# A gated expert on TensorE's column groups, rotations in three operations, and a new order of the first transfers in a state-space kernel

## The chip, the cores and the metric

The kernel runs on one core of one Trainium2 chip. The metric is the time of one execution on the device, in microseconds (us). Two kernels are compared by runs on the same chip, taken in turns. All runs told here gave a correct result. The executions of one kernel in one round spread by 1 to 4 us, and a difference of about 1 us or less is not settled by these runs.

Engines: TensorE (PE in the profile; PEld is its weight loads), VectorE (DVE), ScalarE (ACT), GpSimd (POOL), SyncE (SP). A name such as ACTq is the queue of transfers that this engine issues.

## The reference, cut to what matters

```python
x  = A_x                                  # [1, 2048, 1024], bf16
xn = layernorm(x)
# A: a state-space layer with 1024 complex states, plus a skip
Lam_bar = exp(exp(log_dt) * (Lambda_re + 1j * Lambda_im))
B_bar   = ((Lam_bar - 1) / Lam)[:, None] * (B_re + 1j * B_im)
h[t]    = Lam_bar * h[t-1] + xn[t] @ B_bar.T          # over 2048 tokens
yA      = 2 * (h @ C.T).real + xn * Dskip
# B: one gated expert for the two tokens with the largest r
r   = xn @ w_r
idx = the two largest of r
y   = (silu(xn[idx] @ w_gate) * (xn[idx] @ w_up)) @ w_down * sigmoid(r[idx])   # F = 3584
yB  = xn, with y added at the rows idx
return x + yA + yB
```

## The kernel before

The sequence is cut into 16 chunks of 128 tokens. For each chunk TensorE computes B·x (tile pB), ScalarE copies it out (u), VectorE rotates it (v, four operations), scans it with a real radius (gf), ScalarE casts it (gb), VectorE rotates it back (hT, four operations), and TensorE multiplies by C (pY). VectorE adds the residual (ot). The expert runs between the later chunks.

The order on each engine is fixed when the kernel is built, by a small list scheduler with estimated durations and hand-tuned offsets, cut here:

```python
class Plan:
    def add(self, name, eng, dur, fn, deps=(), key=0.0, takes=(), mb=0.0, lag=0.0): ...
    def run(self): ...     # repeatedly starts the task that can start first; ties by key
    def emit(self): ...    # emits the tasks in that order
```

The start:

```python
nc.scalar.preload_act_table_set("natural_log_exp_and_others")
for c in range(4):                                   # x of chunks 0 to 3, 256 KB each
    (nc.sync if c < 2 else nc.scalar).dma_start(out=xt_tiles[c][:], in_=x2[c * T:(c + 1) * T, :])
prow = moe.tile([5 * PT, 128], BF16, name="prow", tag="row")
for i, src in enumerate((A_Lambda_re, A_Lambda_im, A_log_dt, B_w_r, A_Dskip)):   # 2 KB each
    nc.scalar.dma_start(out=prow[i * PT:(i + 1) * PT, :], in_=src.rearrange("(j i) -> j i", i=128))
# ... after these SyncE issues the transposing loads of B: BT[ri][j], 16 of 256 KB

def par_T():                                         # all five parameters at once
    tab["pP"] = psum.tile([128, 5 * PT], BF16, name="pP", tag="Y", bufs=3)
    nc.tensor.transpose(out=tab["pP"][:], in_=prow[:], identity=ident[0:5 * PT, 0:5 * PT])
```

TensorE's order starts with warm-up products, the transpose of chunk 0 (pT), then pP, pT of chunk 1, and pB. So pP must wait for the last of the five small loads, and everything behind it on TensorE waits with it.

A rotation, and the expert's two inner loops:

```python
def turn_in(c, js=ALLJ):
    # ...
    nc.vector.tensor_tensor(out=m1[:, :, js, :], in0=u, in1=bc(E1c), op=ALU.mult)
    nc.vector.tensor_tensor(out=m2[:, :, js, :], in0=u, in1=bc(E1s), op=ALU.mult)
    nc.vector.tensor_add(out=v[:, 0, js, 2:], in0=m1[:, 0, js, :], in1=m2[:, 1, js, :])
    nc.vector.tensor_sub(out=v[:, 1, js, 2:], in0=m1[:, 1, js, :], in1=m2[:, 0, js, :])

def moe_gateup(n):                                   # 28 visits, 448 products in all
    # ...
    for fl in range(FC // 128):
        ft = fc * (FC // 128) + fl
        for j in range(DT):
            nc.tensor.matmul(out=ms["pG"][:, m, ft, :], lhsT=wt[:, j, fl * 128:(fl + 1) * 128],
                             rhs=ms["xselT"][:, j, :], start=(j == 0), stop=(j == DT - 1))

def moe_down(n):                                     # already in column groups
    # ...
    nc.tensor.matmul(out=ms["pD"][32 * q:32 * q + 2, :], lhsT=ms["guT"][:, ft, :],
                     rhs=wd[:, a, q * DQ:(q + 1) * DQ], ..., tile_position=(0, 32 * q))
```

Of the kernel before, what the change touches and what calls it, by code (L numbers as in the profile page):

```python
# [9 lines left out]
ACT = mybir.ActivationFunctionType  # L10
# [7 lines left out]
T = 128  # L18
# [5 lines left out]
NREP = 4  # L24
ADJUST = {
    ('x', 4): -274.0, ('x', 5): -94.3, ('x', 6): -15.6, ('x', 7): -77.2, ('x', 8): -7.7, ('x', 9): -94.3,
    ('x', 11): -13.0, ('x', 12): -55.3, ('x', 15): -7.1,
    ('B', 0, 0): -906.8, ('B', 0, 1): -906.8, ('B', 1, 0): -986.1, ('B', 1, 1): -986.1, ('B', 2, 0): -728.9,
    ('B', 2, 1): -728.9, ('B', 3, 0): -767.1, ('B', 3, 1): -767.1, ('B', 4, 0): -364.5, ('B', 4, 1): -364.5,
    ('B', 5, 0): -599.0, ('B', 5, 1): -599.0, ('B', 6, 0): -451.9, ('B', 6, 1): -451.9, ('B', 7, 0): -120.1,  # L30
    ('B', 7, 1): -120.1,
    ('C', 0, 0): -47.7, ('C', 0, 1): -47.7,
    ('rstd', 5): 151.6, ('rstd', 10): 59.9,
    ('xnT', 5): -804.0,
    ('sq', 8): 26.9,
    ('apply', 9): 18.3,
    ('sum', 12): -59.1, ('sum', 14): -30.0, ('sum', 15): -21.9,
    ('nmean', 12): 21.0,
    ('nmr', 12): -106.3,
    ('pcol',): 71.2,  # L40
    ('wr',): -7.0,
    ('frq',): 11.2,
    ('ts', 0, 0): -1.2, ('ts', 1, 0): -167.7, ('ts', 0, 1): -1.2, ('ts', 1, 1): -167.7,
    ('E2c', 1): -20.4,
    ('dgD',): -9.1,
    ('u', 0, 0): 22.6, ('u', 0, 1): 22.6, ('u', 0, 2): 22.6, ('u', 0, 3): 22.6, ('u', 0, 4): 22.6, ('u', 0, 5): 22.6,
    ('u', 0, 6): 22.6, ('u', 0, 7): 22.6,
    ('Bu', 4, 0): 52.0, ('Bu', 4, 1): 52.0, ('Bu', 4, 2): 52.0, ('Bu', 4, 3): 52.0, ('Bu', 4, 4): 52.0,
    ('Bu', 4, 5): 52.0, ('Bu', 4, 6): 52.0, ('Bu', 4, 7): 52.0, ('Bu', 5, 0): 110.3, ('Bu', 5, 1): 110.3,
    ('Bu', 5, 2): 110.3, ('Bu', 5, 3): 110.3, ('Bu', 5, 4): 110.3, ('Bu', 5, 5): 110.3, ('Bu', 5, 6): 110.3,  # L50
    ('Bu', 5, 7): 110.3, ('Bu', 6, 0): 125.8, ('Bu', 6, 1): 125.8, ('Bu', 6, 2): 125.8, ('Bu', 6, 3): 125.8,
    ('Bu', 6, 4): 125.8, ('Bu', 6, 5): 125.8, ('Bu', 6, 6): 125.8, ('Bu', 6, 7): 125.8, ('Bu', 7, 0): 186.2,
    ('Bu', 7, 1): 186.2, ('Bu', 7, 2): 186.2, ('Bu', 7, 3): 186.2, ('Bu', 7, 4): 186.2, ('Bu', 7, 5): 186.2,
    ('Bu', 7, 6): 186.2, ('Bu', 7, 7): 186.2,
    ('TI', 0, 0): 1.0, ('TI', 0, 4): 1.0, ('TI', 1, 0): -1.0, ('TI', 1, 4): -1.0, ('TI', 3, 0): -2.4,
    ('TI', 3, 4): -2.4, ('TI', 4, 0): -3.1, ('TI', 5, 0): -3.3,
    ('SC', 0, 0, 0): -8.5, ('SC', 0, 0, 1): -8.5, ('SC', 0, 4, 0): -8.5, ('SC', 0, 4, 1): -8.5,
    ('SC', 3, 0, 0): 38.6, ('SC', 3, 0, 1): 38.6, ('SC', 3, 4, 0): 38.6, ('SC', 3, 4, 1): 38.6,
    ('SC', 5, 0, 0): -51.1, ('SC', 5, 0, 1): -51.1, ('SC', 6, 0, 0): 18.7, ('SC', 6, 0, 1): 18.7,
    ('gb', 0, 0, 0): -13.0, ('gb', 0, 0, 1): -13.0, ('gb', 0, 4, 0): -13.0, ('gb', 0, 4, 1): -13.0,  # L60
    ('TO', 1, 0): -19.8, ('TO', 1, 4): -19.8, ('TO', 4, 0): -85.6, ('TO', 5, 0): 2.5, ('TO', 7, 0): -34.6,
    ('TO', 15, 0): -1.5, ('TO', 15, 4): -1.5, ('TO', 15, 6): -1.5,
    ('cin', 2, 0): -117.9, ('cin', 2, 4): -117.9,
    ('xr', 0): -84.4, ('xr', 1): -75.1, ('xr', 2): -55.1, ('xr', 3): -38.2, ('xr', 4): -53.4, ('xr', 5): -38.7,
    ('xr', 6): -64.2, ('xr', 7): -33.9, ('xr', 8): -35.3, ('xr', 11): -136.6,
    ('Y', 0, 0): 12.6, ('Y', 0, 1): 12.6, ('Y', 0, 2): 12.6, ('Y', 0, 3): 12.6, ('Y', 1, 0): 11.7, ('Y', 1, 1): 11.7,
    ('Y', 1, 2): 11.7, ('Y', 1, 3): 11.7, ('Y', 2, 0): 20.9, ('Y', 2, 1): 20.9, ('Y', 2, 2): 20.9, ('Y', 2, 3): 20.9,
    ('Y', 3, 0): 27.5, ('Y', 3, 1): 27.5, ('Y', 3, 2): 27.5, ('Y', 3, 3): 27.5, ('Y', 9, 0): 121.2,
    ('Y', 9, 1): 121.2, ('Y', 9, 2): 121.2, ('Y', 9, 3): 121.2, ('Y', 10, 0): 157.9, ('Y', 10, 1): 157.9,
    ('Y', 10, 2): 157.9, ('Y', 10, 3): 157.9, ('Y', 12, 0): 192.3, ('Y', 12, 1): 192.3, ('Y', 12, 2): 192.3,  # L70
    ('Y', 12, 3): 192.3, ('Y', 13, 0): 271.5, ('Y', 13, 1): 271.5, ('Y', 13, 2): 271.5, ('Y', 13, 3): 271.5,
    ('out', 2, 0): 14.3, ('out', 2, 1): 14.3, ('out', 8, 0): 81.9, ('out', 8, 1): 81.9,
    ('xa', 5): -18.6,
    ('ADD', 9, 0): 42.2, ('ADD', 9, 1): 42.2,
    ('w', 0): -61.6, ('w', 1): -73.8, ('w', 2): -65.6, ('w', 3): -48.9, ('w', 4): -58.9, ('w', 5): -49.9,
    ('w', 6): -46.1, ('w', 7): -46.5, ('w', 8): -43.0, ('w', 9): -44.6, ('w', 10): -43.9, ('w', 11): -42.3,
    ('w', 12): -45.3, ('w', 13): -45.0, ('w', 14): -44.0, ('w', 15): -44.6, ('w', 16): -45.2, ('w', 17): -45.2,
    ('w', 18): -44.9, ('w', 19): -45.1, ('w', 20): -45.3, ('w', 21): -42.4, ('w', 22): -42.6, ('w', 23): -42.5,
    ('w', 24): -47.4, ('w', 25): -42.6, ('w', 26): -45.3, ('w', 27): -46.3, ('w', 28): -47.2, ('w', 29): -42.6,
    ('w', 30): -39.6, ('w', 31): -43.3, ('w', 32): -27.1, ('w', 33): -39.0, ('w', 34): -14.2, ('w', 35): -24.2,  # L80
    ('w', 36): -15.0,
# [3 lines left out]
class Plan:  # L85
# [3 lines left out]
    FREE = {"PE": 1.35, "DVE": 1.2, "ACT": 4.7, "POOL": 1.8, "SP": 1.65}  # L89
# [80 lines left out]
def kernel(  # L170
# [31 lines left out]
    FC = 256  # L202
    NFC = F // FC
    DQ = D // NREP
    DH = 512
    NDH = D // DH
    x2 = A_x[0]
# [11 lines left out]
    xt_tiles = {c: xin.tile([128, D], BF16, name="xt") for c in range(4)}  # L219
    nc.scalar.preload_act_table_set("natural_log_exp_and_others")  # L220
    for c in range(4):
        (nc.sync if c < 2 else nc.scalar).dma_start(out=xt_tiles[c][:], in_=x2[c * T:(c + 1) * T, :])
    prow = moe.tile([5 * PT, 128], BF16, name="prow", tag="row")
    for i, src in enumerate((A_Lambda_re, A_Lambda_im, A_log_dt, B_w_r, A_Dskip)):
        nc.scalar.dma_start(out=prow[i * PT:(i + 1) * PT, :], in_=src.rearrange("(j i) -> j i", i=128))
# [7 lines left out]
    nc.gpsimd.iota(par_i[:], pattern=[[0, 1]], base=0, channel_multiplier=1)  # L233
    halfpi = consts.tile([128, 1], F32, name="halfpi")
    nc.vector.memset(halfpi[:], math.pi / 2)
    eps_t = consts.tile([128, 1], F32, name="eps_t")
    nc.vector.memset(eps_t[:], EPS)
    first_tok = consts.tile([128, 1], F32, name="first_tok")
# [12 lines left out]
    E1s = consts.tile([128, PT, T], BF16, name="E1s")  # L251
    E2c = consts.tile([128, PT, T], BF16, name="E2c")
# [38 lines left out]
    for c in range(NCH):  # L291
        if c < 4:
            add(("x", c), "none", (3.4, 0.8, 1.5, 0.7)[c], lambda: None, key=c, takes=[("xt", c, [("apply", c)])])
        else:
            add(("x", c), "SP", 0.47 if c > 5 else 1.05, lambda c=c: load_x(c), key=-40 + c, takes=[("xt", c, [("apply", c)])], mb=0.28)
# [106 lines left out]
    NWARM = 36  # L402
    for i in range(NWARM):
        add(("warm", i), "PE", 0.22 if i < 19 else 0.12, keep_clock, [("warm", i - 1)] if i else [], key=100 + i,
            takes=[("pB", "warm", [("warm", NWARM - 1)])])
# [145 lines left out]
    add(("start",), "none", 0.6, lambda: None, key=10)  # L551
# [4 lines left out]
    add(("frq",), "DVE", 0.25, par_frq, [("dt",)], key=-31)  # L556
# [11 lines left out]
    add(("E1s",), "DVE", 0.6, lambda: nc.vector.tensor_copy(out=E1s[:], in_=tab["sf"][:]), [("sin",)], key=-20)  # L568
# [5 lines left out]
    for h, js in enumerate((h0, h1)):  # L574
        for i, (nm, dst) in enumerate((("E2c", E2c), ("E2s", E2s))):
            add(("ts", i, h), "DVE", 0.62, lambda i=i, js=js: table_ts(i, js), [("kappa",), ("sin",)], key=-1.45 + h, takes=[("gb", ("ts", i), [(nm, 1)])])
            add((nm, h), "DVE", 1.05, lambda dst=dst, i=i, js=js: table_E2(dst, i, js), [("ts", i, h), ("cos",)], key=-1.45 + h)
    add(("dgD",), "DVE", 1.2, table_D, [("pcol",)], key=0.1)
    E2D = [(nm, h) for nm in ("E2c", "E2s") for h in range(2)]
    for i in range(3):  # L580
        pl.rings["hT"]["taken"].append((("tab", i), E2D + [("E1c",), ("E1s",), ("ends",)]))
# [53 lines left out]

    def turn_in(c, js=ALLJ):
        n = js.stop - js.start
# [250 lines left out]
    def sel_bn():  # L888
        nc.vector.tensor_scalar_add(out=ms["sig"][:], in0=ms["sig"][:], scalar1=1.0)
        nc.vector.reciprocal(out=ms["sig"][:], in_=ms["sig"][:])  # L890
        ms["mv"] = bn_mean_var(ms["xsel"], 2)
# [142 lines left out]
```

## Time and profile before

| | before |
|---|---|
| time, median of 3 runs | 273.96 us (273.91 to 274.08) |
| span of the profiled execution | 272.3 us |
| TensorE busy | 262.7 us (96%) |
| VectorE busy | 246.1 us (90%) |
| first pB starts | 13.37 us |

The engine table and three rows of the slices, from the profile page of the kernel before. In the engine table, each engine has its busy time and share of the span. In the slices, the span is cut into 40; a digit is tenths, and PEclk is TensorE's granted clock.

```profile
PE 262.7 (96%) x2484; PEld 184.8 (68%) x2504; DVE 246.1 (90%) x360; ACT 145.1 (53%) x239; POOL 107.2 (39%) x204
...
PE   8599999999999999999999999999999999999995
...
DVE  4689999999999999998997999799999998699982
...
PEclk9779999999999999999999999999999999999999
```

TensorE is the fullest engine and VectorE is close. Apart from the last slice, TensorE's only visibly loose slices are at the very start, and there its clock is below full too.

ScalarE's and TensorE's first 14 us of the kernel before, from the timeline (start, length, engine, line, operation, out<-in, count, and in brackets the idle time before it with its releaser; ACTq lines are transfers being issued):

```profile
0.75 0.88 ACTq L222 DMA_DIRECT2D xt<-in_A_x_dram  x2
1.65 0.58 ACTq L225 DMA_DIRECT2D prow<-in_A_Lambda_re_dram  x1
...
5.57 0.28 ACTq L225 DMA_DIRECT2D prow<-in_A_log_dt_dram  x1
7.27 0.30 ACTq L225 DMA_DIRECT2D prow<-in_B_w_r_dram  x1
...
7.96 0.29 ACT L308 ACTIVATE lv<-mv,eps_t 128x1 f32<-128x1 f32 x1 [5.96 <-DMA prow<-in_A_log_dt_dram]
```

```profile
9.13 0.64 PE L385 MATMUL pT<-ident,xn 128*128 128x128 bf16 x8 [1.97 <-DVE xn L358]
11.14 0.19 PE L452 MATMUL pP<-ident,prow 40*128 40x40 bf16 x1 [1.37 <-issue]
...
13.37 1.91 PE L594 MATMUL pB<-xnT,BT 128*128 128x128 bf16 x16
```

ScalarE issued the third and fourth small loads only at 5.57 and 7.27 us, and its first statistic (lv) came behind them. TensorE waited 1.97 us for chunk 0 and 1.37 us before pP, and the first pB started at 13.37 us. The windows view gives the DMA traffic at that time (kernel before; the last two columns are the DMA share and GB/s):

```profile
4.00:6.00 2.00, 2.00 (x21) 2.00 (x20) 1.45 (x4) 0.00 (x0) 0.00 (x0) 1.00 1.12 351
...
10.00:12.00 2.00, 0.86 (x9) 0.84 (x10) 1.97 (x5) 0.82 (x1) 0.40 (x2) 0.50 0.96 188
```

Two groups of the costliest list, kernel before (busy us, mean ns; then idle before):

```profile
L594 PE MATMUL pB<-xnT,BT 128*128 128x256 bf16 (+1 forms) x1040 | 117.9, 272 | 0.0
...
L945 PE MATMUL pG<-xselT,wt 128*128 128x2 bf16 x448 | 13.5, 163 | 0.0
```

The expert's gate and up products (pG) are 448 products of only two moving columns. From start to start, 16 of them take 0.39 us.

### The profile page before, as it was taken

The numbers are of one execution on the slowest core, as the hardware profiler recorded it, in microseconds if no ns is written. First come the engines' busy times: TensorE is split into PE (matmuls) and PEld (weight loads), VectorE is DVE, ScalarE is ACT, GpSimd is POOL, SyncE is SP. The second block draws the span as 40 slices with busy tenths as digits, with TensorE's granted clock in tenths as the row PEclk, the third lists the DMA queues.
The fourth block names the chain that finished last, engine by engine and source line by source line (L and its number), as shares of the span: only waits on it lengthen the run. The fifth ranks groups of instructions, "written<-read, shape, count | busy, mean of one in ns | idle before, by whom it ended". The sixth has DMA issues, their size and how long they took to land.

```text
span 272.3 us, 6159 instructions
## 1 busy us (share of the span) xinstructions
PE 262.7 (96%) x2484; PEld 184.8 (68%) x2504; DVE 246.1 (90%) x360; ACT 145.1 (53%) x239; POOL 107.2 (39%) x204
## 2 busy tenths in 40 slices
PE   8599999999999999999999999999999999999995
PEld 8498898884489555675564896658984577634441
DVE  4689999999999999998997999799999998699982
ACT  1388899996477888996422542214351344213110
POOL 1210066764747563737060196209430515001200
PEclk9779999999999999999999999999999999999999
DMA  6989999998037090714302389969999498632111
GB/s 214 193 180 182 259 199 276 223 268 182 17 96 233 1 195 14 181 42 96 99 0 79 116 231 277 277 188 298 291 264 287 152 337 284 253 137 61 39 39 39
DMA packets 86344, 46.29 MB, mean 170 GB/s; under 512 B 45796, under 2 KB 78570, under 8 KB 86316
## 3 DMA queue, kind: packets, MB, share of 16 engines
q1 hardware_dynamic: 85836, 45.10, 65.9%
q10 hardware_dynamic: 368, 0.53, 0.5%
q8 instruction: 19, 0.31, 0.5%
q0 software_dynamic: 112, 0.27, 0.3%
q14 instruction: 9, 0.07, 0.1%
HBM read 30.68 MB, written 4.20 MB: 128 GB/s over the span
## 4 chain that ended last, share of the span: by engine, by line
PE 49%; DVE 3%; issue 1%
PE pY L774 24%; PE pB L594 17%; PE pG L945 4%; PE pY L767 2%; PE pD L968 1%; DVE gf L666 1%; DVE ot L783 0%; PE pY L776 0%; DVE n L704 0%; DVE n L705 0%; DVE hT L707 0%; PE pI L845 0%; DVE idx L833 0%; DVE top L831 0%; PE pX L905 0%
## 5 line engine op out<-in xcount | busy, mean ns | idle before, releaser
L594 PE MATMUL pB<-xnT,BT 128*128 128x256 bf16 (+1 forms) x1040 | 117.9, 272 | 0.0
L774 PE MATMUL pY<-CT,hT 128*128 128x512 bf16 x492 | 113.9, 379 | 1.3 <-DVE hT L706 0.3
L594 PEld LDWEIGHTS <-BT 128*128 128x128 bf16 x1040 | 99.4, 98 | 12.9 <-issue 0.9
L774 PEld LDWEIGHTS <-hT 128*128 128x128 bf16 x512 | 48.0, 98 | 51.6 <-issue 0.7
L666 DVE TENSOR_TENSOR_SCAN gf<-R,v 128x1040 f32<-128x1040 f32 (+1 forms) x38 | 69.3, 1852 | 0.2 <-POOL v L693 0.2
L682 POOL TENSOR_TENSOR w<-gf,cL 128x8 f32<-128x8 f32 (+1 forms) x38 | 29.0, 763 | 91.7 <-DVE gf L666 79.8
L672 ACT CAST gb<-gf 128x1024 bf16<-128x1024 f32 (+1 forms) x38 | 32.7, 866 | 38.5 <-DVE gf L666 38.3
L600 ACT CAST u<-pB 128x512 bf16<-128x512 f32 x64 | 36.3, 579 | 21.3 <-PE pB L594 21.0
L755 ACT ACTIVATE xa<-xr,nmr_all,rstd_all 128x1024 f32<-128x1024 bf16 x16 | 19.8, 1240 | 35.4 <-DVE ot L783 24.7
L644 DVE TENSOR_TENSOR m<-u,E1c 128x2048 bf16<-128x2048 bf16 (+2 forms) x22 | 20.4, 927 | 6.0 <-ACT u L600 5.5
L783 DVE TENSOR_TENSOR ot<-pY,xa 128x512 bf16<-128x512 f32 x32 | 21.1, 675 | 3.8 <-issue 3.2
L704 DVE TENSOR_TENSOR n<-gb,E2c 128x2048 bf16<-128x2048 bf16 (+2 forms) x22 | 20.4, 926 | 3.8 <-ACT gb L672 3.1
L705 DVE TENSOR_TENSOR n<-gb,E2s 128x2048 bf16<-128x2048 bf16 (+2 forms) x22 | 20.5, 931 | 0.0
L645 DVE TENSOR_TENSOR m<-u,E1s 128x2048 bf16<-128x2048 bf16 (+2 forms) x22 | 20.3, 925 | 0.0
L366 POOL TENSOR_TENSOR nmr_all<-nmean_all,rstd_all 128x1 f32<-128x1 f32 x16 | 8.6, 540 | 29.4 <-ACT rstd_all L309 29.3
L945 PEld LDWEIGHTS <-wt 128*128 128x128 bf16 x448 | 13.5, 96 | 1.9 <-issue 0.2
L683 POOL TENSOR_TENSOR w<-gf,sL 128x8 f32<-128x8 f32 (+1 forms) x38 | 13.9, 367 | 0.0
L344 ACT ACTIVATE xn<-xt,nmean_all 128x1024 bf16<-128x1024 bf16 x12 | 13.8, 1147 | 0.2
L693 POOL TENSOR_TENSOR v<-cy,v 128x16 bf16<-128x16 f32 (+1 forms) x19 | 13.2, 693 | 1.5
L338 ACT ACTIVATE xn<-xt 128x1024 bf16<-128x1024 bf16 x12 | 12.7, 1058 | 1.6 <-DMA xt<-in_A_x_dram 0.9
L945 PE MATMUL pG<-xselT,wt 128*128 128x2 bf16 x448 | 13.5, 163 | 0.0
L362 ACT ACTIVATE xn<-xt,nmr_all,rstd_all 128x1024 bf16<-128x1024 bf16 x10 | 12.4, 1236 | 1.9 <-POOL nmr_all L366 1.8
(137 smaller groups left out, 230.7 us busy)
## 6 DMA issues: line engine op xcount, KB each, us to landing
wt<-in_B_w_up_dram SPq DMA_DIRECT2D x14, 512.0 KB, 4.1
wt<-in_B_w_gate_dram SPq DMA_DIRECT2D x14, 512.0 KB, 6.3
wd<-in_B_w_down_dram SPq DMA_DIRECT2D x14, 512.0 KB, 4.8
xr<-in_A_x_dram SPq DMA_DIRECT2D x16, 256.0 KB, 3.2
out_dram<-ot SPq DMA_DIRECT2D x32, 128.0 KB, 1.7
xt<-in_A_x_dram SPq DMA_DIRECT2D x14, 256.0 KB, 2.9
xt<-in_A_x_dram ACTq DMA_DIRECT2D x2, 256.0 KB, 3.9
xnT<-xn SPq DMA_TRANSPOSE x10, 3.8
```

Of the source, the lines that this page charges most:

```text
L594: nc.tensor.matmul(out=pB[:, ri, ts_], lhsT=BT[ri][j][:, k, :], rhs=xnT_tiles[f][:, k, ts_], start=(k == 0), stop=(k == DT - 1))
L600: nc.scalar.copy(out=u_tiles[f][:, :, j, :], in_=pB_tiles.pop((f, j))[:])
L644: nc.vector.tensor_tensor(out=m1[:, :, js, :], in0=u, in1=bc(E1c), op=ALU.mult)
L645: nc.vector.tensor_tensor(out=m2[:, :, js, :], in0=u, in1=bc(E1s), op=ALU.mult)
L666: nc.vector.tensor_tensor_scan(out=flat(gf), data0=flat(R[:, js, :]), data1=flat(v[:, ri, js, :]), initial=0.0, op0=ALU.mult, op1=ALU.add)
L672: nc.scalar.copy(out=gb_tiles[c][:, ri, js, :], in_=gf_tiles[c, js.start, ri][:, :, 2:])
L682: nc.gpsimd.tensor_tensor(out=w1[:, ri, 0:n], in0=g, in1=cL[:, js], op=ALU.mult)
L704: nc.vector.tensor_tensor(out=n1[:, :, js, :], in0=gb[:, :, js, :], in1=bc(E2c), op=ALU.mult)
L705: nc.vector.tensor_tensor(out=n2[:, :, js, :], in0=gb[:, :, js, :], in1=bc(E2s), op=ALU.mult)
L774: nc.tensor.matmul(out=pY[:], lhsT=h_tiles[c][:, ri, j, :], rhs=CT[ri][dh][:, j, :], start=False, stop=end)
L783: nc.vector.tensor_add(out=y_tiles["ot", c][:, d_], in0=y_tiles.pop(("pY", c, dh))[:], in1=y_tiles["xa", c][:, d_])
L945: nc.tensor.matmul(out=ms["pG"][:, m, ft, :], lhsT=wt[:, j, fl * 128:(fl + 1) * 128], rhs=ms["xselT"][:, j, :], start=(j == 0), stop=(j == ...
```

## The change

The change has five parts.

1. Gate and up products go into TensorE's four column groups: the two tokens (padded to 32) become the stationary operand and the weights the moving one, 256 columns at a time. The result comes out by token, so it is transposed back (pU).
2. The gate's sigmoid is made on ScalarE by Exp, Ln, Exp in place of an add and a reciprocal on VectorE. Rows are scaled on ScalarE.
3. Each rotation takes three VectorE operations over both halves in place of four.
4. The order of the first transfers changes: two small loads first on ScalarE's queue, then x of chunks 2 and 3, then the table load and two more small loads; the fifth small load goes by GpSimd.
5. The scheduler's offsets are tuned anew.

The diff, cut to its core:

```diff
-    nc.scalar.preload_act_table_set("natural_log_exp_and_others")
-    for c in range(4):
-        (nc.sync if c < 2 else nc.scalar).dma_start(out=xt_tiles[c][:], in_=x2[c * T:(c + 1) * T, :])
-    prow = ...
-    for i, src in enumerate((A_Lambda_re, A_Lambda_im, A_log_dt, B_w_r, A_Dskip)):
-        nc.scalar.dma_start(out=prow[i * PT:(i + 1) * PT, :], in_=...)
+    for c in range(2):
+        nc.sync.dma_start(out=xt_tiles[c][:], in_=x2[c * T:(c + 1) * T, :])
+    prow = ...
+    for i in range(2):
+        load_param(nc.scalar, i)
+    for c in range(2, 4):
+        nc.scalar.dma_start(out=xt_tiles[c][:], in_=x2[c * T:(c + 1) * T, :])
     nc.scalar.preload_act_table_set("natural_log_exp_and_others")
+    for i in range(2, 4):
+        load_param(nc.scalar, i)
 # ... after the iotas on GpSimd
+    load_param(nc.gpsimd, 4)
 # ... rotation in (rotation out alike)
-        nc.vector.tensor_tensor(out=m1[:, :, js, :], in0=u, in1=bc(E1c), op=ALU.mult)
-        nc.vector.tensor_tensor(out=m2[:, :, js, :], in0=u, in1=bc(E1s), op=ALU.mult)
-        nc.vector.tensor_add(out=v[:, 0, js, 2:], in0=m1[:, 0, js, :], in1=m2[:, 1, js, :])
-        nc.vector.tensor_sub(out=v[:, 1, js, 2:], in0=m1[:, 1, js, :], in1=m2[:, 0, js, :])
+        nc.vector.tensor_tensor(out=rot, in0=u, in1=both(E1c, js), op=ALU.mult)
+        nc.vector.tensor_tensor(out=m[:, :, js, :], in0=u[:, ::-1], in1=E1s[:, :, js, :], op=ALU.mult)
+        nc.vector.tensor_add(out=rot, in0=rot, in1=m[:, :, js, :])
 # ... gate and up
-                nc.tensor.matmul(out=ms["pG"][:, m, ft, :], lhsT=wt[:, j, fl * 128:(fl + 1) * 128],
-                                 rhs=ms["xselT"][:, j, :], start=(j == 0), stop=(j == DT - 1))
+                for q in range(NREP):
+                    nc.tensor.matmul(out=ms["pG", b][32 * q:32 * q + 32, m, :], lhsT=ms["xselT"][:, j, :],
+                                     rhs=wt[m][:, a, q * fq:(q + 1) * fq], start=(j == 0 and m == 0),
+                                     stop=(j == DT - 1 and m == 1), tile_position=(0, 32 * q))
+        nc.scalar.activation(out=e, in_=ms["pG", b][:, 0, :], func=ACT.Exp, scale=-1.0)
+        nc.scalar.activation(out=e, in_=e, func=ACT.Ln, bias=one_t[:])
+        nc.scalar.activation(out=e, in_=e, func=ACT.Exp, scale=-1.0)
 # ... cut: transposing gu back, the rows on ScalarE, two down steps per visit, the offsets
```

## The prediction

> **What bounds it now.** TensorE: 96% busy in the engine table; VectorE follows with 90%. The chain of waits from 135 us on is almost only TensorE, and in the timeline its groups touch from 13.37 us (first pB) to 268.9 us. Start-to-start there: 16 pB matmuls 1.745 us, 8 pY 1.73, 16 gate/up (pG) 0.39, 8 down (pD) 0.32, 16 pD 0.54. Times count: pB 112 us, pY 118, pG 10.9, pD 4.0. VectorE is a close second until about 130 us (98% of the windows from 20 to 100 us), then has slack.
>
> **Expert.** 448 matmuls of 2 moving columns, each with a 128-column weight load, become 192 of 256 columns and 64 of 128, four to a pass in the column groups. The pD matmuls already run so: (0.54-0.32)/8 = 0.0275 us each, about 0.1 us fixed per visit. Estimate: 12 visits x 0.54 + 2 x 0.95 = 8.2 us, plus 0.4 us for 7 transposes; pairing down steps saves 0.2. Net 2 to 2.5 us, all on TensorE's path. The Trainium skill (TensorEngine Tiling (Array Packing), Key Properties and Restrictions) says that a switch of mode drains the engine, which fits the 0.1 us, and that column tiling excludes fast weight load: 32-column loads may hide less well than pD's 2-column ones. No trace here shows that yet; it is my main doubt.
>
> **Gate.** Three activations in each of 4 blocks, two VectorE products and a copy: about 2.5 us more VectorE, but the row scalings (1.9 us) leave it. Off the path.
>
> **Rotations.** A full one takes about 3.7 us start-to-start; three operations of 2048 about 3.45. A half goes from 2.0 to 1.9. VectorE sheds 5 to 7 us; that only keeps it level with a TensorE that starts earlier.
>
> **Start.** ScalarE computed the first rstd only at 7.96 us although its statistics were ready at 6.05: it was issuing small parameter loads that waited for earlier landings (issued at 5.57, 7.27, 7.60 us). TensorE waited until 11.1 us for the last ("issue" before pP), was idle from 7.1 to 9.1, and its granted clock was 0.5 from about 10 to 16 us. Now the last parameter goes by GpSimd, the others wait for x0 and x1 (about 4.5 and 5.9 us), and more warm matmuls fill the gap. I expect rstd at 6.3, apply at 7.5, pP near 9.3, first pB at 10 to 11 instead of 13.4, at a higher clock (the skill, TensorE: Matmul & The Clock Gate, Part 1: an idle window halves it; the 0.5 here agrees). Worth 2.5 to 4.5 us to TensorE; VectorE starts its tables only about 2 us earlier, so I take back 1 to 2 us as waits of pY for hT between 50 and 100 us.
>
> **Sum.** 273.96 - 2.3 (expert) - 3.5 (start) - 0.7 (fewer small gaps) + 1.2 (waits for hT) = 268.7; a looser order later may give 0.7: **268.0 us, range 264.8 to 271.2.** Faster by over 2% (under 268.5): 0.56; within: 0.42; slower: 0.02.
>
> **Right or wrong shows in:** first pB start; PEclk in slices 2 and 3; start-to-start of 16 pG (0.54); mean of the 2048-element VectorE operations (1.22 us; the reversed halves must not slow them); idle of pY for hT; end of pD to the first hot-row matmul.
>
> **Wrong if** weight loads make a pG visit 0.8 us or more; parameters land after 10.5 us; VectorE can't feed the earlier pY, so the start gain is lost; weights (42 x 0.5 MB at about 260 GB/s) arrive late and hold pY of the last chunks.

## The result, and the profile after

| | before | after |
|---|---|---|
| median | 273.94 us (273.33 to 274.08, 4 runs) | 270.94 us (270.67 to 271.65, 4 runs) |
| ratio | | 0.9899, interval 0.9873 to 0.9924 |
| span of the profiled execution | 272.3 | 269.4 us |
| first pB starts | 13.37 us | 11.79 us |
| first pY of C·h starts | 60.11 us | 54.21 us |
| last product with the hot rows starts | 268.55 us | 265.60 us |
| VectorE busy | 246.1 us | 243.6 us |

A ratio is the mean time of one kernel's runs over that of the other's in the same rounds, so it is not quite the ratio of the medians quoted. Where kernels of different rounds are compared below, the ratios are compared, and a ratio step of 0.001 is taken as 0.27 us.

The gain is 3.0 us (1.0% by ratio) where 6.0 us (2.2%) were predicted. The same rows of the profile page, kernel after:

```profile
PE 259.0 (96%) x2298; PEld 177.3 (66%) x2321; DVE 243.6 (90%) x322; ACT 153.2 (57%) x257; POOL 105.5 (39%) x205
...
PE   7599999999999999999999999999999999999994
...
DVE  5598999999999989999998979998988999999952
...
PEclk9989999999999999999999999999999999999999
```

The second slice of TensorE (about 6.7 to 13.5 us) is still half empty. The timeline of the start, kernel after, ScalarE and then TensorE:

```profile
0.72 0.59 ACTq L230 DMA_DIRECT2D prow<-in_A_Lambda_re_dram  x1
...
1.66 0.84 ACTq L235 DMA_DIRECT2D xt<-in_A_x_dram  x2
...
3.63 0.32 ACTq L230 DMA_DIRECT2D prow<-in_A_log_dt_dram  x1
4.24 0.30 ACTq L230 DMA_DIRECT2D prow<-in_B_w_r_dram  x1
5.20 0.30 ACT L324 ACTIVATE lv<-mv,eps_t 128x1 f32<-128x1 f32 x1 [1.38 <-DVE mv L348]
```

```profile
7.24 0.61 PE L401 MATMUL pT<-ident,xn 128*128 128x128 bf16 x8
...
11.22 0.18 PE L468 MATMUL pP<-ident,prow 40*128 40x40 bf16 x1 [3.03 <-DMA prow<-in_B_w_r_dram]
...
11.79 5.46 PE L612 MATMUL pB<-xnT,BT 128*128 128x128 bf16 x48
```

ScalarE's side came out as forecast: w_r was issued at 4.24 us in place of 7.27, and the first statistic at 5.20 in place of 7.96. Chunk 0 was transposed at 7.24 in place of 9.13. But the 2 KB of w_r were there only at 11.2 us, 7.0 us after their issue. TensorE sat idle for 3.03 us before pP, which started no earlier than before (11.22 against 11.14). The first 48 pB then took 5.46 us; at full clock they take 3.7 to 3.9 (old_start and gpsimd_old_gateup below). The windows view of the kernel after:

```profile
4.00:6.00 2.00, 2.00 (x23) 2.00 (x22) 1.97 (x5) 0.50 (x2) 0.37 (x2) 1.00 1.04 142
...
14.00:16.00 2.00, 2.00 (x16) 1.60 (x15) 1.97 (x4) 1.03 (x3) 1.91 (x4) 0.50 0.88 185
```

From 4 to 6 us the DMA engines moved 142 GB/s where the kernel before moved 351, though they count as no less busy (share 1.04 against 1.12). And the clock (the last column but two) is at 0.50 from 14 to 16 us.

The chain of waits by engine and its largest lines, kernel after, then before (shares of the span):

```profile
PE 55%; DVE 25%; ACT 8%; DMA 5%; POOL 3%; issue 2%; SPq 0%; DVEq 0%
```

```profile
PE 49%; DVE 3%; issue 1%
```

After the change the chain of waits passes through VectorE for a quarter of the span (from about 24 to 105 us in the chain listed by time), and through the load of w_r. The two chains cannot be compared share by share: that of before covers only 53% of the span, its later part, where VectorE has slack.

The gate and up products, kernel after, with shapes apart:

```profile
L974 PE MATMUL pG<-wt,mw 128*32 128x256 bf16 x192 | 7.1, 275 | 0.0
...
L974 PE MATMUL pG<-wt,mw 128*32 128x128 bf16 x64 | 1.3, 220 | 0.0
```

### The profile page after: what moved, and what is told of

Same layout as the page of the kernel before. It is cut to its first block, busy times and chain, and to the rows that moved or that the text cites. A ratio compares the mean times of both kernels' runs of the same rounds, so it can differ in the third digit from the quotient of the medians.

```text
span 269.4 us, 5756 instructions
## 1 busy us (share of the span) xinstructions
PE 259.0 (96%) x2298; PEld 177.3 (66%) x2321; DVE 243.6 (90%) x322; ACT 153.2 (57%) x257; POOL 105.5 (39%) x205
## 4 chain that ended last, share of the span: by engine, by line
PE 55%; DVE 25%; ACT 8%; DMA 5%; POOL 3%; issue 2%; SPq 0%; DVEq 0%
PE pY L789 28%; PE pB L612 19%; DVE gf L684 8%; PE pG L974 3%; DVE v L663 3%; DVE m L664 3%; DVE v L665 3%; DMA prow<-in_B_w_r_dram 3%; PE pY L782 2%; DVE hT L722 2%; DVE m L721 2%; DVE hT L720 2%; ACT xn L378 2%; PE pD L1013 1%; DVE ot L798 1%
## 5 line engine op out<-in xcount | busy, mean ns | idle before, releaser
L700 POOL TENSOR_TENSOR w<-gf,cL 128x8 f32<-128x8 f32 (+1 forms) x38 | 30.1, 791 | 89.1 <-DVE gf L684 89.0
L720 DVE TENSOR_TENSOR hT<-gb,E2c 128x2048 bf16<-128x2048 bf16 (+2 forms) x22 | 20.4, 926 | 1.4 <-ACT gb L690 1.2
L663 DVE TENSOR_TENSOR v<-u,E1c 128x2048 bf16<-128x2048 bf16 (+2 forms) x22 | 20.4, 927 | 1.4 <-ACT u L618 1.2
L665 DVE TENSOR_TENSOR v<-v,m 128x2048 bf16<-128x2048 bf16 (+2 forms) x22 | 20.7, 941 | 0.8
L722 DVE TENSOR_TENSOR hT<-hT,m 128x2048 bf16<-128x2048 bf16 (+2 forms) x22 | 20.7, 939 | 0.8
L721 DVE TENSOR_TENSOR m<-gb,E2s 128x2048 bf16<-128x2048 bf16 (+2 forms) x22 | 20.5, 931 | 0.0
L382 POOL TENSOR_TENSOR nmr_all<-nmean_all,rstd_all 128x1 f32<-128x1 f32 x16 | 9.3, 583 | 17.2 <-ACT rstd_all L325 17.2
L710 POOL CAST v<-cy 128x16 bf16<-128x16 f32 (+1 forms) x19 | 10.0, 526 | 7.6 <-DVE gf L684 6.4
```

The source lines that it names most:

```text
L663: nc.vector.tensor_tensor(out=rot, in0=u, in1=both(E1c, js), op=ALU.mult)
L665: nc.vector.tensor_add(out=rot, in0=rot, in1=m[:, :, js, :])
L700: nc.gpsimd.tensor_tensor(out=w1[:, ri, 0:n], in0=g, in1=cL[:, js], op=ALU.mult)
L720: nc.vector.tensor_tensor(out=rot, in0=g, in1=E2c[:, :, js, :], op=ALU.mult)
L721: nc.vector.tensor_tensor(out=m[:, :, js, :], in0=g[:, ::-1], in1=both(E2s, js), op=ALU.mult)
L722: nc.vector.tensor_add(out=rot, in0=rot, in1=m[:, :, js, :])
```

## The experiments

The expectations name their theories each in their own words; in this text they are numbered. T1: the lost part of the gain is the late landing of w_r, caused by the new order of transfers. (Below, "overlap" is short for one thing: x2 and x3 are issued beside or behind the first transposing load of B, not ahead of it. It means the order of issue. In time the copies and the transposes run together in every kernel here: even in x_on_sp of round 4, where the first transpose goes out latest of all, at 2.60 us, x2 and x3 are issued from 1.65 us and land no sooner than 2.6 us later.) Rivals: T2, the gate and up products in column groups cost more than thought; T3, the rotations gave VectorE nothing, and VectorE holds everything; T4, ScalarE's queue itself is slow for small loads.

### Round 1: undo one part each

**old_gateup**: the changed kernel with gate and up as products of two moving columns.

```diff
-                for q in range(NREP):
-                    nc.tensor.matmul(out=ms["pG", b][32*q:32*q+32, m, :], lhsT=ms["xselT"][:, j, :],
-                                     rhs=wt[m][:, a, q*fq:(q+1)*fq], ..., tile_position=(0, 32*q))
+                for s_ in range(ns):
+                    nc.tensor.matmul(out=ms["pG", b][:, m, s_, :], lhsT=wt[m][:, a, s_*128:(s_+1)*128],
+                                     rhs=ms["xselT"][:, j, 0:2], ...)
```

> The changed kernel with gate and up put back to matmuls of 2 moving columns with 128-column weight loads, on the same weight tiles and at the same places of the schedule. Theory A (TensorE bounds, the expert is on its path): the 448 short matmuls take about 0.78 us a visit instead of 0.56, the 7 transposes go; time up by 2.6 to 3.6 us on the changed kernel's 270.9, to 273.5 to 274.5. Theory B (after about 130 us something else ends last, such as the weight transfers or the last rows): under 1 us more.

Measured: 271.76 us, ratio 0.9949 (0.9914 to 0.9984). Against the changed kernel (0.9899, and 0.9894 in a later repeat) that is 1.4 us slower, but by medians only 0.8, so neither forecast is met (2.6 to 3.6, or under 1). The column groups gain; how much, round 2 shows with a steadier start. T2, as a loss, falls. Its profiled execution was the fastest of its six (269.9 us), and there pP started at 8.86 us, though its start is the changed kernel's. So the landing of w_r varies from run to run with this start.

**old_rotations**: the changed kernel with rotations in four operations and no negated table halves.

```diff
-        nc.vector.tensor_tensor(out=rot, in0=u, in1=both(E1c, js), op=ALU.mult)
-        nc.vector.tensor_tensor(out=m[...], in0=u[:, ::-1], in1=E1s[:, :, js, :], op=ALU.mult)
-        nc.vector.tensor_add(out=rot, in0=rot, in1=m[...])
+        (the four operations of the kernel before; rotation out alike)
```

> The changed kernel with the rotations in four VectorE operations again and without the negated tables. Theory A (TensorE alone bounds): under 1 us more than 270.9. Theory B (VectorE is the bound up to about 105 us, as the chain of the changed kernel has it): each half costs about 0.1 us and each whole rotation about 0.25 us more there, 2 to 4 us in all up to 105 us, so 273 to 275.

Measured: 271.93 us, ratio 0.9925 (0.9895 to 0.9955), about 0.8 us slower than the changed kernel by ratio; its profile had pP at 11.65 us. One such step is at the limit of what these runs settle; it is taken up below.

**old_start**: the changed kernel with the first transfers as before.

```diff
-    for i in range(2): load_param(nc.scalar, i)
-    for c in range(2, 4): nc.scalar.dma_start(out=xt_tiles[c][:], ...)
     nc.scalar.preload_act_table_set(...)
-    for i in range(2, 4): load_param(nc.scalar, i)
+    for c in range(2, 4): nc.scalar.dma_start(out=xt_tiles[c][:], ...)
+    for i in range(5): load_param(nc.scalar, i)
-    load_param(nc.gpsimd, 4)
```

> The changed kernel with the start's transfers issued as before (activation table, x2, x3, five parameters on ScalarE's queue, nothing on GpSimd's). Theory A (the new order moved the start's real gate, the landing of the last parameter, not at all: 11.1 us before, 11.2 us after): the first rstd comes at about 8 us again, the first pB at 12.5 to 13.4 us, time up by no more than 1.5 us. Theory B (the new start is worth the 3.5 us that was predicted): up by 3 us or more.

Measured: 269.15 us, ratio 0.9843 (0.9813 to 0.9872). It is faster than the changed kernel: the new order of transfers, which was to bring 3.5 us, loses about 1.5 us. In its profile w_r is issued at 7.2 us, three microseconds later than in the changed kernel, and yet pP starts at 10.04 and the first pB at 10.76, at full clock. ScalarE's queue and TensorE in this kernel:

```profile
7.17 0.30 ACTq L230 DMA_DIRECT2D prow<-in_B_w_r_dram  x1
```

```profile
10.04 0.18 PE L465 MATMUL pP<-ident,prow 40*128 40x40 bf16 x1
```

The kernel before issues its transfers alike, with the first pB at 13.37. So 2.6 us of an earlier first pB (2.1 by the profile of all_undone below) come without any change of transfers.

**params_gpsimd**: the changed kernel with x of chunks 2 and 3 first on ScalarE's queue, and all five small loads on GpSimd's.

```diff
-    for i in range(2): load_param(nc.scalar, i)
     for c in range(2, 4): nc.scalar.dma_start(out=xt_tiles[c][:], ...)
     nc.scalar.preload_act_table_set(...)
-    for i in range(2, 4): load_param(nc.scalar, i)
-    load_param(nc.gpsimd, 4)
+    for i in range(5): load_param(nc.gpsimd, i)
```

> The changed kernel with all five parameters issued by GpSimd at about 1.6 to 5.3 us; x2, x3 and the table stay on ScalarE's queue. Theory A (the late landing of w_r, 6.9 us after its issue behind x2 and x3 on the same queue, holds both TensorE and VectorE's tables): the last parameter lands by about 8.5 us, first pB at 9 to 10 us instead of 11.8, time down by 2 to 3 us to about 268.4. Theory B (the start is absorbed later): within 0.7 us of 270.9. Theory C (any small load waits for the transposes, whatever its queue): it lands at about 11 us again, no change.

Measured: 268.55 us, ratio 0.9825 (0.9794 to 0.9856), the lowest median. The small loads landed 4.2 to 4.6 us after issue, pP started at 8.90 and the first pB at 9.74 us. This is the start that the prediction described, and the time is near its 268.0. But against old_start (0.9843) it gains only 0.5 us by ratio, which these runs don't settle.

This run shows that a start as predicted takes back the loss of about 2 us, but it changes two things at once: the queue of the small loads, and the place of x2 and x3.

### Round 2: which of the two, and the other parts with a steady start

**x_first**: the changed kernel with x2 and x3 ahead of the two small loads on ScalarE's queue; nothing else.

```diff
-    for i in range(2): load_param(nc.scalar, i)
     for c in range(2, 4): nc.scalar.dma_start(out=xt_tiles[c][:], ...)
+    for i in range(2): load_param(nc.scalar, i)
```

> The changed kernel with one thing moved: x2 and x3 go to ScalarE's queue ahead of the two small parameter loads, not behind them; everything else of the new start stays (table after, last parameter by GpSimd). Theory A (x2 and x3 issued 0.9 us later run beside the first transposes, and w_r behind them then lands 7 us after its issue in most runs): x2, x3 issued at 0.7 to 1.6 us, w_r lands by about 8 to 9.5 us, no idle of 3 us before pP, granted clock stays 1.0, time 268.5 to 269.5 against 270.9. Theory B (w_r is slow for another reason): pP at 11 us again, 270.5 or more.

Measured: 269.13 us, ratio 0.982 (0.9788 to 0.9852), 2 us better than the changed kernel by ratio. The place of two transfers is enough. Its profile, of the slowest of its five executions (270.1 us), has w_r issued at 7.2 and pP at 10.12 us: later than the forecast landing, because the issue is late, but at most 2.9 us after it. The traffic from 4 to 6 us is back, windows view of this kernel:

```profile
4.00:6.00 2.00, 2.00 (x36) 2.00 (x35) 1.29 (x2) 0.00 (x0) 0.00 (x0) 1.00 1.12 347
```

**gpsimd_old_gateup**: params_gpsimd with the edit of old_gateup, so that the expert is weighed with a steady start.

> The kernel with all parameters by GpSimd (268.55 us), with gate and up put back to matmuls of 2 moving columns. The start no longer hides anything, so this is the worth of the column groups. Theory A (all of their TensorE time is on the path: 11.3 us of matmuls in place of 7.75 + 0.4): up by 2.5 to 3.3 us, to 271.0 to 271.9. Theory B (part of it is slack or is paid back by drains at each visit): up by 1 to 2 us.

Measured: 270.68 us, ratio 0.9891 (0.9857 to 0.9924). Against params_gpsimd the column groups gain 2.1 us by medians, 1.8 by ratios. From start to start in the two traces, the pG take 7.75 us in place of 11.22, the transposes back add 0.38, the down products 0.23, and the pB beside the visits 0.71 us: a net of 2.15 us.

**gpsimd_old_rotations**: params_gpsimd with the edit of old_rotations.

> The kernel with all parameters by GpSimd (268.55 us), with four-operation rotations. Theory A (VectorE is the bound up to about 100 us once the start is early): up by 2 to 4 us. Theory B (TensorE sets the pace, as old_rotations with only 1 us over the changed kernel says): up by under 1.2 us.

Measured: 269.93 us, ratio 0.9856 (0.9822 to 0.9889); params_gpsimd gains 0.8 us on it by ratios, 1.4 by medians, and its VectorE is busy for 243.0 us in place of 246.9. The product that starts the choice of the tokens came at 121.80 us here and at 120.23 in params_gpsimd, 1.57 us later. VectorE's timeline of one rotation out, this kernel (the last line starts the next operation):

```profile
113.41 1.23 DVE L719 TENSOR_TENSOR n<-gb,E2c 128x2048 bf16<-128x2048 bf16 x1
114.56 1.22 DVE L720 TENSOR_TENSOR n<-gb,E2s 128x2048 bf16<-128x2048 bf16 x1
115.81 0.69 DVE L721 TENSOR_TENSOR hT<-n,n 128x1024 bf16<-128x1024 bf16 x1
116.42 0.68 DVE L722 TENSOR_TENSOR hT<-n,n 128x1024 bf16<-128x1024 bf16 x1
117.02 4.53 DVE L682 TENSOR_TENSOR_SCAN gf<-R,v 128x1040 f32<-128x1040 f32 x2
```

The same in the kernel after:

```profile
114.31 1.22 DVE L720 TENSOR_TENSOR hT<-gb,E2c 128x2048 bf16<-128x2048 bf16 x1
115.45 1.24 DVE L721 TENSOR_TENSOR m<-gb,E2s 128x2048 bf16<-128x2048 bf16 x1
116.73 1.24 DVE L722 TENSOR_TENSOR hT<-hT,m 128x2048 bf16<-128x2048 bf16 x1
117.89 4.53 DVE L684 TENSOR_TENSOR_SCAN gf<-R,v 128x1040 f32<-128x1040 f32 x2
```

This pair is nearly even: 3.61 us against 3.58. The mean over the full rotations between 30 and 130 us is 3.67 us for four operations (seven in this kernel) and 3.53 for three (seven in params_gpsimd), so one full rotation saves about 0.14 us, not the 0.25 of the prediction. Reading `u[:, ::-1]` or writing in place costs nothing here: the operations stay at 1.22 to 1.24 us. The saving can show in the total because VectorE is on the chain up to about 105 us. T3 falls, though a gain of 0.8 to 1.4 us is at the limit of what the runs settle.

**pP_late**: the changed kernel with pP moved behind the first pB products in TensorE's order, so that TensorE needn't idle for w_r.

```diff
-    pl.run().emit()
+    pl.run()
+    later(("pP",), ("Bu", 0, 0)); later(("pcol",), ("pP",))
+    later(("dt",), ("rstd", 3)); later(("frq",), ("apply", 3))
+    pl.emit()
```

> The changed kernel with its start's transfers untouched, but the parameter transpose pP behind the first eight pairs of pB groups in TensorE's order, and its users on VectorE and ScalarE behind the statistics of chunks 2 and 3. Theory A (what costs is TensorE's own idle of 3 us before pP and the cold clock after it): first pB at 9.5 to 10.5 us, time down by 1.5 to 2.5 us. Theory B (what costs is VectorE's table chain, which starts at the landing whatever TensorE does): under 0.7 us gained, with pY or pB then waiting on VectorE or ScalarE before 100 us.

Measured: 270.3 us, ratio 0.9852 (0.9816 to 0.9889), 1.1 to 1.3 us better than the changed kernel by ratio but only 0.3 to 0.6 by medians. TensorE started pB at 9.33 us, earlier than in params_gpsimd, but pP came at 11.64. VectorE's tables for the rotations are made from pP's result, so they came no earlier than in the changed kernel, and the time stayed above that of params_gpsimd. That fits a loss that is not TensorE's idle time alone, with VectorE held by late parameters too. It does not show it: pP waited for nothing in this run, so it was late by its new place in the order and not by the landing of w_r, and the edit moves two users of pP as well.

### Round 3: the queue, the spread, and the kernel before

**after_again**: the changed kernel unaltered.

> The changed kernel itself once more, as the neighbour of the next runs. Theory A (its start is unsteady: w_r landed by 8.9 us in one profile of this start, at 11.2 and 11.7 in two others): 270 to 272, with single executions spread over 1.5 us or more. Theory B (steady): all within 0.5 us of 270.9.

Measured: 270.57 us, ratio 0.9894 (0.9866 to 0.9922): the result repeats. The profiled execution was its fastest (269.5 us), with pP at 10.49 us. Over four profiles with this start (after, after_again, old_gateup, old_rotations), pP started at 11.22, 10.49, 8.86 and 11.65. The landing is not only late but unsteady. Every pP and first pB told here is of one execution, the profiled one, and not of the median.

**late_by_gpsimd**: the first transfers as in the changed kernel, but the last three small loads on GpSimd's queue, so w_r is issued at 2.33 us.

```diff
-    for i in range(2, 4): load_param(nc.scalar, i)
-    load_param(nc.gpsimd, 4)
+    for i in range(2, 5): load_param(nc.gpsimd, i)
```

> The changed kernel with log_dt and w_r issued by GpSimd as well, so that no small load stands behind x2 and x3 on ScalarE's queue; x2 and x3 still go out behind two small loads, beside the first transposes. Theory A (w_r is late because it stands behind x2 and x3 on that queue): the last parameter lands by 8.5 us, time 268.5 to 269.3. Theory B (x2 and x3 beside the transposes slow every transfer, whatever its queue): it lands at 9.5 us or later in the profile, time 269.7 or more.

Measured: 270.33 us, ratio 0.9885 (0.9851 to 0.9919), the same as the changed kernel. One line of GpSimd's timeline and one of TensorE's, this kernel:

```profile
2.33 0.53 POOL L230 DMA_DIRECT2D prow<-in_B_w_r_dram  x1
```

```profile
10.67 0.18 PE L467 MATMUL pP<-ident,prow 40*128 40x40 bf16 x1 [2.51 <-DMA prow<-in_B_w_r_dram]
```

Issued 1.9 us earlier and by another queue, w_r still held pP until 10.67 us. T4 falls: neither the queue nor the time of issue is the cause.

**before_params**: the kernel before, with its five small loads on GpSimd's queue and nothing else.

```diff
-    for i, src in enumerate(...): nc.scalar.dma_start(out=prow[...], ...)
 # ... after the iotas on GpSimd
+    for i, src in enumerate(...): nc.gpsimd.dma_start(out=prow[...], ...)
```

> The kernel before with one thing changed: its five parameters go by GpSimd. Theory A (the start of the kernel before was held by their landing and by ScalarE's issuing of them): first rstd at about 6.3 us, pP near 9 us, first pB at 10 to 11.5 us, down by 1.5 to 3 us against the kernel before. Theory B (its start is held by its instruction order or by VectorE later): under 0.8 us.

Measured: 273.21 us, ratio 0.9976 (0.9943 to 1.0008), the same as the kernel before. In its profile the first pB started at 10.08 us in place of 13.37, and at full clock. But the first pY of C·h came at 58.95 us in place of 60.11, so of 3.3 us of lead only 1.2 were left. Of the 2.1 us lost, 1.5 went into two waits of TensorE for ScalarE (0.42 us before 29.5 and 1.09 before 36.6 us). In the old order an earlier TensorE is worth 0.7 us by ratio, as Theory B had it, and not more than 1.6 by the interval.

**all_undone**: the changed kernel with old_gateup, old_rotations and old_start together. What is left of the change is the new order, the split of visits, the gate in three activations and the rows on ScalarE.

> The changed kernel with its three named parts all undone at once (2-column gate and up, four-operation rotations, transfers of the start issued as before): what is left is the new order of the instructions, the split of the expert into 14 visits and 4 gates, and the rows on ScalarE. If the parts add up (269.15 with the old start, 2.1 for the gate and up, 1.4 for the rotations): 272.3 to 273.0, so 1 us or so of the gain is the new order alone. If they don't add: 271.5 or less, or 273.5 or more.

Measured: 273.17 us, ratio 0.9982 (0.9956 to 1.0008): about 0.5 us better than the kernel before, within its interval of zero. It lies between the two forecasts, so it does not settle whether the parts add up.

### Round 4: overlap, or lateness alone

Open after round 3: x2 and x3 in the changed kernel are issued at 1.66 us in place of 0.75, beside the first transposing load of B (issued at 1.65) and not ahead of it. Is it this place beside the transpose (the overlap, as said above) that slows all transfers, or only that x2 and x3 are issued late? The two kernels of this round issue them as late as the changed kernel, but ahead of the transposes on the same queue.

**x_on_sp**: the changed kernel with x2 and x3 on SyncE's queue.

```diff
-        nc.scalar.dma_start(out=xt_tiles[c][:], in_=x2[c * T:(c + 1) * T, :])    # c = 2, 3
+        nc.sync.dma_start(out=xt_tiles[c][:], in_=x2[c * T:(c + 1) * T, :])
```

> The changed kernel with one thing different: the copies of x2 and x3 go out on SyncE's queue behind x1 and ahead of the transposes of the scan's factors[...]. The parameters stay on ScalarE, three of them behind its table load as in the change. Theory A (the copies running beside the first transposes slow every transfer, the small w_r load with them): w_r lands by about 9 us, TensorE's product of the parameters (pP) starts before 9.6, the granted clock stays at 1.0 past 10 us, 268.5 to 269.7. Theory B (what costs is that x2 and x3 are issued late at all, or that w_r is issued late on ScalarE): pP at 10.5 or later, 270.3 to 271.

Measured: 269.31 us, ratio 0.9824 (0.9795 to 0.9852), 1.9 to 2.0 us better than the changed kernel. From its timeline, SyncE, ScalarE and TensorE:

```profile
1.65 0.91 SPq L235 DMA_DIRECT2D xt<-in_A_x_dram  x2
2.60 1.34 SPq L299 DMA_TRANSPOSE BT<-in_A_B_re_dram  x1
```

```profile
2.02 0.32 ACTq L230 DMA_DIRECT2D prow<-in_B_w_r_dram  x1
```

```profile
7.67 0.19 PE L468 MATMUL pP<-ident,prow 40*128 40x40 bf16 x1
...
8.50 2.98 PE L612 MATMUL pB<-xnT,BT 128*128 128x128 bf16 x40
...
12.80 1.05 PE L612 MATMUL pB<-xnT,BT 128*128 128x256 bf16 x8 [1.32 <-DMA BT<-in_A_B_im_dram]
```

pP waited for nothing and started at 7.67 us, 3.5 us earlier than in the changed kernel, at full clock. The DMA engines moved 281 GB/s from 4 to 6 us. One thing moved that the edit did not intend: w_r is issued at 2.02 us, earlier than the changed kernel's 4.24. late_by_gpsimd issued it at 2.33 and still got it at 10.67. But there it stood behind the first transpose (1.65), and here it stands ahead of it (2.60), so this run alone leaves a rival: that a small load lands early when it goes out ahead of the transposes. The next run settles that. Part of the lead is given back: the transposes, now 1 us later, hold pB for 1.6 us in all. So this kernel is level with params_gpsimd by ratio.

**x_on_sp_gpsimd**: the same place for x2 and x3, and all small loads by GpSimd.

> The same place for x2 and x3 (SyncE's queue, ahead of the transposes), and all five parameters from GpSimd's queue. Beside params_gpsimd (268.55), which has x2 and x3 early on ScalarE's queue. Theory A: no overlap with the transposes in either, so pP near 8.5 to 9.2 and 268.2 to 269.3, the same as params_gpsimd. Theory B: x2 and x3 come later than there, so the start is late again: pP at 10 or later, 270 or more.

Measured: 269.69 us, ratio 0.9863 (0.9825 to 0.9901), pP at 7.79 us. GpSimd's queue and TensorE, this kernel:

```profile
3.37 0.52 POOL L230 DMA_DIRECT2D prow<-in_B_w_r_dram  x1
```

```profile
7.79 0.18 PE L465 MATMUL pP<-ident,prow 40*128 40x40 bf16 x1
```

Here w_r goes out behind the first transpose (2.60), and pP is as early as in x_on_sp. So neither the lateness of x2 and x3 nor the place of w_r makes the landing late. What does is the place of x2 and x3 against the first transposing load. For this kernel that rests on the profile: by ratio it is only 0.6 us better than late_by_gpsimd (0.9885), which the runs don't settle. The time lies between the two forecasts (268.2 to 269.3, or 270 and more); two of its six executions took 271 and 272 us, for a reason that these runs don't show. The queue of the small loads brings nothing once the overlap is gone.

### All runs

| kernel | median us | ratio to before | pP, us | first pB, us |
|---|---|---|---|---|
| before | 273.94 | 1 | 11.14 | 13.37 |
| after | 270.94 | 0.9899 | 11.22 | 11.79 |
| after_again | 270.57 | 0.9894 | 10.49 | 11.05 |
| old_gateup | 271.76 | 0.9949 | 8.86 | 9.50 |
| old_rotations | 271.93 | 0.9925 | 11.65 | 12.22 |
| old_start | 269.15 | 0.9843 | 10.04 | 10.76 |
| params_gpsimd | 268.55 | 0.9825 | 8.90 | 9.74 |
| x_first | 269.13 | 0.9820 | 10.12 | 10.68 |
| pP_late | 270.30 | 0.9852 | 11.64 | 9.33 |
| late_by_gpsimd | 270.33 | 0.9885 | 10.67 | 11.24 |
| x_on_sp | 269.31 | 0.9824 | 7.67 | 8.50 |
| x_on_sp_gpsimd | 269.69 | 0.9863 | 7.79 | 8.56 |
| gpsimd_old_gateup | 270.68 | 0.9891 | 8.93 | 9.76 |
| gpsimd_old_rotations | 269.93 | 0.9856 | 8.95 | 9.78 |
| before_params | 273.21 | 0.9976 | 8.84 | 10.08 |
| all_undone | 273.17 | 0.9982 | 10.73 | 11.30 |

The version that beats both kernels is the change with x2 and x3 kept ahead of the transposes: params_gpsimd, x_first and x_on_sp have ratios of 0.9825, 0.9820 and 0.9824, which these runs don't tell apart. Nor do they tell them from old_start (0.9843, 0.9813 to 0.9872): to leave the transfers as they were is within 0.6 us of the best start tried.

## Why the prediction was right or wrong

**In sum.** The time predicted was 268.0 us and the range 264.8 to 271.2; 270.94 lies inside it, at its upper end. The gain was half of what was predicted (3.0 us against 6.0), and "faster by over 2%", given 0.56, did not come.

The runs give the change as a path of three steps, each a difference of ratios: new order and offsets alone, −0.5 us (all_undone); column groups and three-operation rotations on top, −3.8 us (old_start against all_undone); the new order of transfers on top, +1.5 us (the changed kernel against old_start). That is −2.8 us.

**The step that failed: the start.** The prediction said: "Now the last parameter goes by GpSimd, the others wait for x0 and x1 (about 4.5 and 5.9 us) ... I expect rstd at 6.3, apply at 7.5, pP near 9.3, first pB at 10 to 11 instead of 13.4, at a higher clock", and put −3.5 us into the sum. ScalarE's part of it was right: the loads were issued at 3.63 and 4.24 us, and the first rstd was made at 5.52. What failed first is the silent step from issue to landing. The landing was taken to be about as quick as before (w_r then took 11.14 − 7.27 = 3.9 us at most), but took 7.0 us. Of the 3.0 us gained in its issue time (7.27 to 4.24) nothing was left at pP: 11.22 against 11.14. What the runs showed in its place: moving x2 and x3 behind two small loads puts them beside the first transposing loads; there the traffic from 4 to 6 us falls from 351 to 142 GB/s, and small loads land late and unsteadily. x_first and x_on_sp put the copies ahead again in two ways and both repair it. late_by_gpsimd changes queue and issue time, keeps the overlap and doesn't. TensorE's idle stretch became 3.0 us, and its clock fell to 0.5 again, against "at a higher clock". As a term of the sum, this part is +1.5 us and not −3.5 + 1.2.

The worth of the start was mis-sized as well. Against old_start, even params_gpsimd, whose pP and first pB came earlier than predicted, is only 0.5 us faster by ratio.

The prediction did name "parameters land after 10.5 us" among what would make it wrong. It gave that case too little weight, because it looked at what ScalarE's sequencer waited for and not at what x2 and x3 would now run beside.

**With the start as predicted, the sum came close partly by luck.** params_gpsimd, with pP at 8.90 and the first pB at 9.74 us, took 268.55 us. By ratio that is a gain of 4.8 us against the 6.0 predicted, and it is made otherwise: about 0.5 from the new order, 3.8 from column groups and rotations and 0.5 from the transfers. The sum had 2.3 for the expert, nothing for the rotations, 2.3 for the start (3.5 − 1.2) and 1.4 for small gaps and a looser order.

**The expert: right, or nearly.** Predicted 2 to 2.5 us net; measured 1.8 to 2.1 with a steady start, 0.8 to 1.4 with the unsteady one. 16 products of 256 columns took 0.55 us per visit (predicted 0.54). The doubt about 32-column weight loads did not come true. The Trainium skill (TensorEngine Tiling (Array Packing), Restrictions) says that column tiling disables fast weight load; in this trace the loads still hid behind products in four groups. The visits with 128 columns, for which 0.95 us were allowed, took 0.56. The drain at a switch of mode (same page, Key Properties) may be a small part that the prediction did not count beyond its 0.1 us per visit: the pB beside the visits took 0.71 us more in all. That the drain is the reason is not shown.

**The gate: not weighed.** No run puts it back alone: both kernels of each comparison for the expert have it. all_undone, which has it too, is not slower than the kernel before, so a large loss on the path is unlikely.

**The rotations: off.** Predicted: VectorE sheds 5 to 7 us, "that only keeps it level with a TensorE that starts earlier", so no term in the sum. Measured: with the rotations alone changed, VectorE is busy for 3.7 to 3.9 us less (247.3 against 243.6, 246.9 against 243.0), only 0.14 us for a full rotation, but 0.7 to 1.6 us of the time (ratios of two pairs, and the milestone at 120 us). VectorE was on the chain up to about 105 us, so part of a smaller saving counted. That the reversed halves stay at 1.22 us was predicted, and the Trainium skill (VectorE: DVE Perf Modes, The perf-mode tier table) has the same figure for two bf16 inputs, 1224 ns for 2048 elements.

**Waits of pY for hT:** 1.2 us were taken back for them. The profile after has 0.5 us, and 0.6 of pB for u. With an earlier start (params_gpsimd) they are 0.5 and 0.4. The term was too large by about 0.7 us for the waits it names. Against that, the 0.7 us for small gaps and the 0.7 for a looser order have only the 0.5 us of all_undone to show, which lies within its interval of zero.

**Why an earlier start is worth so different amounts.** before_params started pB 3.3 us earlier and gained nothing that the runs settle; params_gpsimd started 2.0 us earlier than the changed kernel and gained 2 us. In the old order most of the lead went into waits for ScalarE. That the new order has the tables and the rotations ready for it is argued and not tested. pP_late fits: TensorE early and the parameters late kept only part of the gain. How much the clock does is open too. In all_undone the granted clock averaged 0.997 over its six executions, where the kernel before averaged 0.992 over its eleven of the same round, and the ratio is only 0.9982. But of the 44 executions of the kernel before in the four rounds, the 13 with a clock of 0.994 or more have a median of 273.4 us and the 18 at 0.988 or less one of 274.4. So about 1 us goes with the clock, and whether the clock or an earlier start makes it, these runs don't show.

**Still open.** Why the place of two copies against the first transpose slows the transfers, and why the landing varies from 8.9 to 11.7 us with one and the same start, the runs don't show. Why x_on_sp_gpsimd has two long executions is open as well.

## What to carry to other kernels

When a change reorders the first transfers, list for each one what it will run beside, not only when it is issued: here a 2 KB load issued three microseconds earlier landed no earlier, because two 256 KB copies had moved beside a transposing load. It is worth trying to put plain copies that are needed early ahead of the first transposing load. Check the landing of the last small load on the critical path by the wait of its first user. Compare with the old order of transfers inside the new kernel, as old_start did: it was within 0.6 us of the best. Before counting an earlier start of one engine as gain, look whether the next engine on the chain starts earlier too.

## What the Trainium skill lacked or had wrong

- Copies beside transposing loads. DMA: Bandwidth & Descriptors, Rules for kernel authors, says "A transpose next to ordinary DMAs needs nothing". For correctness all runs agree. For speed the page lacks the cost: with 0.5 MB of copies issued beside the first transposes in place of ahead of them, the traffic from 4 to 6 us was 127 to 216 GB/s in six profiles (lowest late_by_gpsimd, highest old_gateup), against 281 to 351 in the ten others (lowest x_on_sp).
- The latency of small loads. The same page, Anatomy of one DMA, gives about 2.0 us fixed per transfer on GpSimd's path. Here, in the busy first 10 us, 2 KB loads by GpSimd took 3.5 to 5.1 us from issue to landing with the copies ahead of the transposes, and 4.7 to 7.7 with the overlap.
- That spreading transfers over queues only saves issue time (same page, Rules for kernel authors) agrees: small loads on another queue changed nothing while the overlap lasted (270.33 us against 270.57).
- Column groups. TensorEngine Tiling (Array Packing), Restrictions, lists what column tiling disables, but not what that costs in a visit like this. Here 16 products of 256 columns with 32-column weight loads took 0.55 us, and 32 of 128 columns 0.56, so the loads hid; the pB next to the visits took 0.71 us more over the whole expert.
- That an earlier TensorE can be worth little (before_params: 3.3 us earlier, ratio 0.9976) belongs to no page; it is a property of this kernel's chain.
